# A fused mLSTM and feed-forward kernel on one core: the first steps' decay matrices by a triangular product and exp, three weight tensors signed by a Prelu slope, and a new order of the front

## The chip, the cores and the metric

The kernel runs on one core of a Trainium2 chip. Its engines are named as the profile names them: PE (TensorE, with PEld for its weight loads), DVE (VectorE), ACT (ScalarE), POOL (GpSimd) and SP (SyncE, which here only issues transfers). The metric is the device time of one run in microseconds, as the median of several runs. Beside it stands one profiled execution, from which every row comes.

## The reference

Two parts follow each other. The first is an mLSTM recurrence for 4 x 8 heads over 768 positions, with vectors of 40:

```python
m_new = np.maximum(f_gate[:, :, t] + m, i_gate[:, :, t])
f_stab = np.exp(f_gate[:, :, t] + m - m_new)
i_stab = np.exp(i_gate[:, :, t] - m_new)
C = f_stab * C + i_stab * outer(v, k);  n = f_stab * n + i_stab * k
y[:, :, t] = sigmoid(o_gate[:, :, t]) * (C @ q) / np.maximum(np.abs(n @ q), 1.0)
```

The second takes y as 3072 tokens of 320, and computes `softplus(x @ w_in) @ w_out` with 2048 hidden units. The two weight arrays arrive as 64-bit floats.

## The kernel before

The work is cut into 24 steps of 128 positions of one batch entry (8 heads each), and into 8 tiles of 3 steps. For each tile, `products` runs 16 blocks of 128 hidden units: eight matmuls of `wih`/`wil` with X into a bank `hp` (L1007), the softplus on ACT (L879 for tile 0, L883 after it), then the products with w_out into `po` (L978). There are three `hp` banks. X is the step's output, split into a high and a low part.

A step needs the decay from position s to position t, which is the product of f over the positions in between. `decay` (L449) gets it on DVE with one scan along t for four heads, from a row of f broadcast over the partitions and an identity that starts each row at 1. The scores are weighed with it (`weigh`, L584), `values` multiplies by the gated values (`vi`, L473, on POOL) into `yp` (L628), takes the reciprocal of the norm (`nq`), scales the output gate (`og`, L635, on POOL), writes `x` (L638, L639), and `split_x` transposes it (L733) and makes X high on ACT (L735) and X low on DVE (L737).

Weights are decoded from 64-bit words to single floats in `single`: ACT makes the magnitude (`mag`, L220), ACT or POOL takes the last three mantissa bits from the low word's top byte (`sg`, L225 or L228, by the parity of a number in `Q`), ACT writes the sign half (L230), and DVE joins the two (L233). Each w_in tensor is then split into a high part on ACT (L257, L261) and a low part on DVE (L265, L267). The first three tensors are decoded ahead of the products. Raw weights have three buffers.

What happens before the first product (the front) is `first_tile`: three steps whose pieces are emitted in the order of the numbers in the dictionary `F`. Every engine and the SP queue run their instructions in the order of emission. The pieces named below are `g0`, `g1` (the first gates: load, then the scan for m, the exps and the transpose of the input gate into `gT`), `lg0` to `lg2` (the gates of the later positions: load, scan, exp), `l0` to `l2` (q, k, v of a step), `f0` to `f2` and `sc0` to `sc2` (decay rows, scans), `s`, `m` (scores, weighing), `vi`, `v0a` to `v2c` (values), `x0a` to `x2c` (X), `wp` (one piece of the decoding of weights each), `wm` (seven warm-up matmuls), `o0s` and `o1s` (sigmoids of the output gates), `tsig` and `tab` (loads of ACT's function tables), `fz` (the decay rows of the first positions to DRAM, `gz_d`), and `zs` (zeros of state buffers, on POOL). In steps 0 and 1 the decay rows are broadcast by PE: one column of the identity, repeated, times `fg0`, per head (L437). Step 2 reads its rows back from `gz_d`.

After the first product, pieces are released by a count of matmuls n (a tile is 272 counts): steps 3 to 5 at `B3`, `B4`, `B5` with the offsets in `M`, later steps with those in `N` and `W`, and the decoding of the other weight tensors with `CI`, `CO`, `CS`, `K0`, `K1`.

Of the kernel before, what the change touches and what calls it, by code (L numbers as in the profile page):

```python
# [44 lines left out]
def mlstm_moe_kernel(  # L45
# [243 lines left out]
    W = dict(FB=-89, LOAD=-66, Y=-28, SCAN=10, VI=-5, VW=14, IQ=14, SP=23, SPD=12, CN=35, CD=36, CE=38, CF=68, YQ=52,  # L289
             YQD=4, EV=1, YD=66, YD1=-16, RD=96, RY=10, RZ=2, NM=132, FIN=137, XH=24, XL=4)  # L290
    M = dict(FB=-25, LOAD=-59, Y=13, SCAN=17, VI=-5, VW=17, IQ=37, SP=24, SPD=5, CN=35, CD=49, CE=54, CF=39, YQ=39,
             YQD=-22, EV=0, YD=41, YD1=-18, RD=85, RY=-6, RZ=0, NM=108, FIN=114, XH=8, XL=-4, CP=39)
    N = dict(FB=-26, LOAD=-59, Y=-6, SCAN=9, VI=-11, VW=11, IQ=23, SP=28, SPD=8, CN=30, CD=36, CE=38, CF=49, YQ=54,
             YQD=6, EV=1, YD=60, YD1=-4, RD=84, RY=-38, RZ=16, NM=125, FIN=150, XH=-9, XL=11)
    Q = dict(Gi0=-3, Go0=0, Gi1=0, Go1=1, Gi2=0, Go2=1, Gi3=0, Go3=17, Gi4=4, Go4=4, Gi5=-2, Go5=-1, Gi6=0, Go6=1,
             Gi7=0, Go7=1, B3=12, B4=71, B5=141, B6=232, B7=265, B8=372, B9=444, B10=525, S0=-377, S1=-292, S2=-199,
             GT=-393, GL=52, LB=217, LS=39, SPD=1, OF0=1, OF1=19, GR0=5, GR1=31, GR2=13, GR3=14, GR4=-3, GR5=27,
             LG=44, FS0=-23, FS1=-6, FSW=8, CI=-50, CO=-3, CS=34, K0=-8, K1=-17, CF=15, RC=-27, RS=95, B2=9, B11=617,
             GT2=92, GL2=106, FS2=0, GR6=-4)
    CI = dict(A=2, B=-14, C=6, D=24, E=19, F=32)  # L300
    CO = dict(A=18, B=-8, C=16, D=27, E=45)

    F = dict(wm=16, zs=212, g0=10, l0=19, w00=46, l1=51, g1=31, fz=63, o0=118, l2=116, lg0=7, f2=118, o1=122, o2=315,
             w10=210, w01=126, f0=163, s0=150, f1=146, s1=210, vi0=196, sc0=226, ld0=230, m00=254, m01=230, wp0=280,
             o0s=223, wp1=210, vi1=244, sc1=254, ld1=273, m10=285, m11=277, wp2=308, lg1=60, lg2=77, tsig=76,
             o1s=323, sc2=262, ld2=275, v0a=274, s2=317, v1a=312, v0b=358, tab=320, m20=330, v0c=404, m21=312,
             vi2=298, v2a=370, v1b=345, wp3=358, x0a=459, x0b=414, v1c=424, x1a=441, v2b=456, x0c=437, wp4=428,
             wp5=405, wp6=300, wp7=300, wp8=305, wp9=328, wp10=432, wp11=434, wp12=371, wp13=369, wp14=362, wp15=436,
             wp16=437, fetch2=348, fetch3=437, fetch=490, x1b=480, x1c=492, v2c=407, x2a=526, x2b=511, x2c=512,
             wr=512, sv0=526, sv1=536, sv2=660, tk6=153, tk5=155, tk4=160, tk3=165, tk2=162, tk1=174)  # L310
# [800 lines left out]
```

## Time and profile before

| what | us |
|---|---|
| median of 3 runs (471.85 to 472.82) | 471.95 |
| the profiled execution | 468.21 |
| its span, first to last instruction | 466.4 |
| PE busy in the span | 441.0 (95%) |
| DVE busy | 312.1 (67%) |
| ACT busy | 214.1 (46%) |
| POOL busy | 121.3 (26%) |

The busy times are means over the whole span. The front, which the change rewrites, is its first tenth, and there the shares are different. The profiled execution took 3.7 us less than the median of the other runs.

### The profile page before, as it was taken

What the parts mean: (1) busy time and instruction counts of PE and PEld (TensorE: products, weight loads), DVE (VectorE), ACT (ScalarE), POOL (GpSimd) and SP (SyncE); (2) the same over time, 40 slices, a digit from 0 to 9 for tenths busy, and PEclk for the clock granted to TensorE, in tenths of its full rate; (3) what the DMA queues carried; (4) which work ended last, traced back from release to release, by engine and by line L of the source; (5) the groups of instructions that cost most, each with busy time, mean ns of one, the idle gap of its engine ahead of it and who ended that gap; (6) DMA issues with size and microseconds to landing.
All of it is one profiled execution on the core that took longest, in us unless ns stands there. A gap on an engine that the chain in (4) does not pass through costs nothing.

```text
span 466.4 us, 10338 instructions
## 1 busy us (share of the span) xinstructions
PE 441.0 (95%) x4173; PEld 412.8 (89%) x4173; DVE 312.1 (67%) x585; ACT 214.1 (46%) x413; POOL 121.3 (26%) x137
## 2 busy tenths in 40 slices
PE   7487978998999999999999999999999999999997
PEld 6375866776999999999999999999999999999996
DVE  5855856989788877875776867756877687332121
ACT  5398557774343633354433633363334442433332
POOL 6415252546321332143031322212313111000000
PEclk9755998999999999999999999999999999999999
DMA  6948296977727643643562464354364220101001
GB/s 202 333 149 237 100 244 205 298 198 182 200 77 184 173 112 129 185 135 89 154 190 84 109 190 130 104 154 123 117 191 120 87 73 20 40 3 44 1 0 44
DMA packets 38399, 63.07 MB, mean 135 GB/s; under 512 B 5486, under 2 KB 20278, under 8 KB 38350
## 3 DMA queue, kind: packets, MB, share of 16 engines
q1 hardware_dynamic: 26218, 54.13, 39.8%
q10 hardware_dynamic: 12132, 8.26, 6.3%
q8 instruction: 33, 0.54, 0.5%
q14 instruction: 16, 0.13, 0.1%
HBM read 54.07 MB, written 8.31 MB: 134 GB/s over the span
## 4 chain that ended last, share of the span: by engine, by line
PE 72%; DMA 9%; DVE 8%; issue 4%; ACT 3%; SPq 1%; POOL 1%; ACTq 0%; DVEq 0%; POOLq 0%
PE hp L1007 33%; PE po L978 31%; PE yq L668 4%; DMA vt<-in_vko 2%; DMA yd<-y 2%; DMA gz_d<-fg 2%; PE sp L616 2%; PE sp L610 1%; DMA fc<-fc_d 1%; DMA yx<-yd 1%; DMA wi<-in_wts 1%; DVE pw L449 1%; DMA fb<-gz_d 1%; DVE nm L712 1%; ACT gh L883 1%
## 5 line engine op out<-in xcount | busy, mean ns | idle before, releaser
L1007 PE MATMUL hp<-X,wih 128*128 128x384 f32 x768 | 183.5, 346 | 3.2 <-ACT X L723 1.2
L1007 PEld LDWEIGHTS hp<-X,wih 128*128 128x128 f32 x768 | 135.5, 189 | 7.1 <-ACT X L723 1.6
L883 ACT ACTIVATE gh<-hp 128x384 fp32r<-128x384 f32 x112 | 55.1, 492 | 182.1 <-PE hp L1007 174.4
L887 DVE TENSOR_TENSOR gl<-hp,gh 128x384 fp32r<-128x384 f32 x112 | 61.7, 554 | 51.1 <-ACT hp L884 49.9
L978 PE MATMUL po<-woh,gl 128*128 128x320 f32 x336 | 72.2, 313 | 0.0
L978 PE MATMUL po<-wol,gh 128*128 128x320 f32 x336 | 71.2, 311 | 0.0
L978 PE MATMUL po<-woh,gh 128*128 128x320 f32 x336 | 70.2, 309 | 0.0
L1007 PE MATMUL hp<-X,wil 128*128 128x384 f32 x256 | 66.5, 341 | 0.0
L496 POOL TENSOR_TENSOR vw<-vt,gw 128x328 f32<-128x328 f32 x23 | 21.7, 944 | 144.5 <-DVE gw L487 137.8
L978 PEld LDWEIGHTS po<-woh,gh 128*128 128x128 f32 x336 | 57.3, 188 | 0.1
L978 PEld LDWEIGHTS po<-woh,gl 128*128 128x128 f32 x336 | 55.0, 189 | 0.6
L978 PEld LDWEIGHTS po<-wol,gh 128*128 128x128 f32 x336 | 54.5, 188 | 0.3
L884 ACT ACTIVATE hp<-hp 128x384 f32<-128x384 f32 x112 | 54.4, 486 | 0.0
L574 POOL TENSOR_TENSOR v<-v,flast 40x328 f32<-40x328 f32 x32 | 30.5, 953 | 63.7 <-DVE v L577 33.6
L1007 PEld LDWEIGHTS hp<-X,wil 128*128 128x128 f32 x256 | 46.8, 189 | 0.3
L621 DVE TENSOR_TENSOR mv<-sp,pw 64x256 f32<-64x256 f32 x72 | 27.2, 417 | 15.8 <-PE sp L616 15.5
L978 PE MATMUL po<-wof,gh 128*128 128x320 f32 x96 | 30.2, 459 | 4.4 <-DVE wof L233 4.4
L376 DVE TENSOR_TENSOR mv<-mv,fc 64x512 f32<-64x512 f32 (+1 forms) x36 | 31.0, 862 | 0.6
L478 POOL TENSOR_TENSOR v<-vt,gT 64x328 f32<-64x328 f32 x36 | 28.6, 794 | 9.0 <-DMA vt<-in_vko 6.5
L978 PEld LDWEIGHTS po<-wof,gh 128*128 128x128 f32 x96 | 18.5, 200 | 12.0 <-DVE wof L233 5.3
L725 DVE TENSOR_TENSOR X<-eg,X 128x384 fp32r<-128x384 f32 x21 | 12.2, 583 | 24.9 <-ACT X L723 24.8
L577 DVE TENSOR_TENSOR v<-v,sp 40x164 f32<-40x164 f32 x64 | 20.7, 323 | 2.4 <-POOL v L574 0.9
(133 smaller groups left out, 488.5 us busy)
## 6 DMA issues: line engine op xcount, KB each, us to landing
qk<-in_qk SPq DMA_DIRECT2D x21, 416.0 KB
vt<-in_vko SPq DMA_DIRECT2D x23, 324.0 KB
wi<-in_wts SPq DMA_DIRECT2D x8, 640.0 KB
wo<-in_wts SPq DMA_DIRECT2D x8, 640.0 KB
fb<-fz_d SPq DMA_DIRECT2D x36, 128.0 KB
eg<-in_oT SPq DMA_DIRECT2D x7, 576.0 KB
out<-ob SPq DMA_DIRECT2D x24, 160.0 KB
yd<-y ACTq DMA_DIRECT2D x36, 96.0 KB
```

Source lines behind the costliest of these rows:

```text
L376: nc.vector.tensor_tensor(z.mv[ch][r], z.mv[ch][r], z.fc[r], op=ALU.mult)
L478: nc.gpsimd.tensor_tensor(vi, v1[r], g[r], op=ALU.mult)
L496: nc.gpsimd.tensor_tensor(z.vw, v1, z.gw.broadcast_to([128, H, E]), op=ALU.mult)
L574: nc.gpsimd.tensor_tensor(heads(whole), old, f, op=ALU.mult)
L577: nc.vector.tensor_tensor(dst[i], dst[i], z.cps[ch][dims(i)], op=ALU.add)
L621: nc.vector.tensor_tensor(half(z.mv[ch][r], i), sps[i][r], half(z.pw[r], i), op=ALU.mult)
L668: nc.tensor.matmul(yq[i * PP : i * PP + m, p, rows(ch)], z.v[ch][k, h * E : h * E + m], z.mv[ch][k, h, :], start=True, stop=True,)
L883: nc.scalar.activation(gh, hp, AF.Softplus)
L884: nc.scalar.activation(hp, hp, AF.Softplus)
L887: nc.vector.tensor_tensor(gl, hp, gh, op=ALU.subtract)
L978: nc.tensor.matmul(po[j], a[:, j * 128 : (j + 1) * 128], w, start=first, stop=(last and left[j] == 0))
L1007: nc.tensor.matmul(hp, a, r, start=(i == 0), stop=(i == len(seq) - 1))
```

## The change

Decay matrices of steps 0, 1 and 2. The logarithm of f is transposed (`lT`). For each step and each half of the heads, POOL writes a tile that holds the logarithm of position s at all t not before s, and 0 elsewhere (`affine_select`, pieces `r`). PE multiplies it by a strictly triangular matrix `later`, which sums the logarithms, ACT takes the exp, and POOL sets the other half to 0 (pieces `e`). The scans, the broadcasts by PE, and step 2's trip through `gz_d` are gone. The steps take their next pieces from one generator, so the four of a step run in the order of their numbers, whatever their names.

Weights. For the three tensors decoded ahead, `mag` is a Prelu whose slope puts the sign into the exponent's top bit; the third ACT instruction goes. For the others, the low parts of w_in can go to POOL by the parity of `H` and `J` in `Q`; three pairs (`Ji0`, `Ji2`, `Ji4`) do.

Order. The new numbers put the load of the first gates first in the SP queue, `lg0`, all of the steps' loads, the output gates and two weight tensors behind it, the selects and exps of all three steps ahead of all scores, `tsig` behind the last exp, and `o1s` ahead of `tab`. So the tables are loaded once each. `zs` goes behind the third X. The numbers of the later steps change a little, and with `EV=-1` the copy of `y` in steps 3 to 5 goes from DVE to ACT.

```diff
+    later = p1.tile([128, 4, 128], F32, tag="fc", name="later")[:, 0]
+    nc.gpsimd.memset(later, 1.0)
+    nc.gpsimd.affine_select(
+        later, later, pattern=[[-1, 128]], compare_op=ALU.is_gt, fill=0.0, base=0, channel_multiplier=1
+    )
...
+        nc.vector.memset(fg[:, 0:1], 0.0)
         nc.scalar.activation(ig, ig, AF.Exp)
+        pg = ps_a.tile([128, 2, NCHAIN], F32, tag="pa", name="pg0")
+        nc.tensor.transpose(pg[:, 1], fg, ident[:NCHAIN, :NCHAIN])
+        nc.tensor.transpose(pg[:, 0], ig, ident[:NCHAIN, :NCHAIN])
+        nc.scalar.copy(lT, pg[:, 1])
+        nc.scalar.copy(gT[:, 0, :], pg[:, 0])
+        done.add(("gT", 0))
+        yield
         nc.scalar.activation(fg, fg, AF.Exp)
         nc.vector.memset(fg[:, 0:1], 0.0)
         done.add("fg0")
-        pg = ps_a.tile([128, NCHAIN], F32, tag="pa", name="pg0")
-        nc.tensor.transpose(pg, ig, ident[:NCHAIN, :NCHAIN])
-        nc.scalar.copy(gT[:, 0, :], pg)
-        done.add(("gT", 0))
         yield
...
-        nc.scalar.activation(mag, hi_w.bitcast(F32), AF.Copy, scale=2.0**-112)
+        if slope:
+            nc.scalar.activation(mag, hi_w.bitcast(F32), AF.Prelu, scale=2.0**-112, alpha=-(2.0**32))
+        else:
+            nc.scalar.activation(mag, hi_w.bitcast(F32), AF.Copy, scale=2.0**-112)
...
+        if slope:
+            nc.scalar.activation(sg, top, AF.Copy, scale=1.0 / 32, bias=-31.0 / 64)
+        elif Q["G" + n] % 2:
...
-        nc.scalar.activation(half[:, :, 1], hi_w.bitcast(F32), AF.Copy, scale=2.0**-112)
-        yield
+        if not slope:
+            nc.scalar.activation(half[:, :, 1], hi_w.bitcast(F32), AF.Copy, scale=2.0**-112)
+            yield
...
-        nc.vector.tensor_tensor(wil[:, :, cs], w2, wih[:, 0:2, cs], op=ALU.subtract)
+        e0, e1 = (nc.gpsimd if Q[k + f"i{u}"] % 2 else nc.vector for k in "HJ")
+        e0.tensor_tensor(wil[:, :, cs], w2, wih[:, 0:2, cs], op=ALU.subtract)
         for d, x, y in los:
-            nc.vector.tensor_tensor(d, x, y, op=ALU.subtract)
+            e1.tensor_tensor(d, x, y, op=ALU.subtract)
...
+    M = dict(FB=-25, LOAD=-47, Y=3, SCAN=14, VI=-15, VW=17, IQ=31, SP=24, SPD=21, CN=35, CD=51, CE=67, CF=45, YQ=39,
+             YQD=-50, EV=-1, YD=45, YD1=-15, RD=85, RY=-27, RZ=0, NM=113, FIN=114, XH=8, XL=-4, CP=39)
...
+    F = dict(wm=140, zs=820, g0=-20, l0=12, w00=118, l1=88, g1=145, fz=297, o0=109, l2=85, lg0=82, f2=226, o1=308,
+             o2=684, w10=181, w01=298, f0=192, s0=304, f1=224, s1=308, vi0=364, ld0=328, m00=352, m01=361, wp0=444,
+             o0s=437, wp1=492, vi1=368, ld1=365, m10=368, m11=369, wp2=499, lg1=244, lg2=280, tsig=423, o1s=726,
+             ld2=396, v0a=448, s2=399, v1a=468, v0b=473, tab=750, m20=398, v0c=492, m21=408, vi2=418, v2a=548,
+             v1b=492, wp3=503, x0a=515, x0b=560, v1c=524, x1a=594, v2b=586, x0c=603, wp4=552, wp5=577, wp6=588,
+             wp7=576, wp8=664, wp9=665, wp10=712, wp11=699, wp12=746, wp13=765, wp14=851, wp15=862, wp16=877,
+             fetch2=685, fetch3=764, fetch=572, x1b=589, x1c=623, v2c=591, x2a=700, x2b=685, x2c=706, wr=850,
+             sv0=774, sv1=782, sv2=780, tk6=720, tk5=760, tk4=728, tk3=784, tk2=812, tk1=810, r0=178, r1=180, r2=183,
+             e00=196, e01=188, e10=227, e11=236, e20=246, e21=246, g2=278)
...
-            need("fg0" if z.s < 2 else ("gz", z.c))
+            need(("gz", z.c))
             z.fbs = []
             for i in range(2):
-                if z.s >= 2:
-                    fb = p2.tile([128, HG, L], F32, tag="fb", name=f"fb{z.n}_{i}")
-                    nc.sync.dma_start(fb, gz_d[z.c, z.hs].rearrange("(i p) t -> i p t", i=2)[i].partition_broadcast(128))
-                    z.fbs.append(fb)
-                    continue
-                fb = ps_h.tile([128, HG, L], F32, tag="hp", name=f"fb{z.n}_{i}")
-                for j in range(HG):
-                    h = z.b * H + i * HG + j
-                    nc.tensor.matmul(
-                        fb[:, j, :], ident[:, h : h + 1].broadcast_to([128, 128]), fg0, start=True, stop=True
-                    )
+                fb = p2.tile([128, HG, L], F32, tag="fb", name=f"fb{z.n}_{i}")
+                nc.sync.dma_start(fb, gz_d[z.c, z.hs].rearrange("(i p) t -> i p t", i=2)[i].partition_broadcast(128))
                 z.fbs.append(fb)
...
+    def first_decays(z):
+
+        need(("gT", 0))
+        z.pws = []
+        keep = dict(compare_op=ALU.is_ge, fill=0.0, base=0, channel_multiplier=-1, pattern=[[0, HG], [1, L]])
+        for i in range(2):
+            pw = p2.tile([128, HG, L], F32, tag="pw" if z.s < 2 else "fb", name=f"pw{z.n}_{i}", **({"bufs": 4} if z.s < 2 else {}))
+            g = half(lT[:, z.hs], i).unsqueeze(2).broadcast_to([128, HG, L])
+            nc.gpsimd.affine_select(pw, g, **keep)
+            z.pws.append(pw)
+        yield
+        fbs = []
+        for i in range(2):
+            fb = ps_h.tile([128, HG, L], F32, tag="hp", name=f"fb{z.n}_{i}")
+            nc.tensor.matmul(fb, later, z.pws[i], start=True, stop=True)
+            fbs.append(fb)
+        yield
+        for i in range(2):
+            nc.scalar.activation(z.pws[i], fbs[i], AF.Exp)
+            nc.gpsimd.affine_select(z.pws[i], z.pws[i], **keep)
+            yield
...
+            done.add("softplus")
...
+            yield from (weights_out if i else weights)(u, words and "softplus" not in done)
```

## Rows read from the trace of the kernel before

**Rows 1.** Page, 40 slices of the span: busy tenths of PE, TensorE clock granted.
```profile
PE   7487978998999999999999999999999999999997
...
PEclk9755998999999999999999999999999999999999
```

**Rows 2.** Windows: us; busy time of PE, PEld, DVE, ACT, POOL; clock, DMA share, GB/s.
```profile
80.00:100.00 20.00, 18.19 (x126) 14.28 (x127) 18.25 (x32) 16.31 (x29) 10.15 (x8) 1.00 0.81 253
```

**Rows 3.** Waits of PE, 39 to 140 us: us in total, times, longest.
```profile
PE po L978 <- DVE wof L233: 4.4, 3, 2.5
```

**Rows 4.** Timeline, 0 to 25 us: start us, us, engine, line, op, idle before.
```profile
1.19 0.41 SPq L158 DMA_DIRECT2D ig<-in_gates  x1
...
2.10 0.42 SPq L133 DMA_DIRECT2D ig<-in_gates  x1
...
2.49 3.35 PE L750 MATMUL wm<-ident 128*128 128x128 f32 x14 [2.49 <-POOL ident L78]
...
3.95 0.47 DVE L136 TENSOR_TENSOR_SCAN m<-fg,m,ig 32x128 f32<-32x128 f32 x1 [2.95 <-DMA ig<-in_gates]
...
6.12 0.19 ACT L147 COPY gT<-pg 128x32 f32<-128x32 f32 x1 [0.33 <-PE pg L146]
...
6.33 1.28 ACT L790 ACT_TABLE_LOAD   x1
...
7.61 1.28 ACT L167 ACT_TABLE_LOAD   x1
...
9.76 1.16 PE L437 MATMUL fb<-fg,ident 128*128 128x128 f32 x8
...
15.67 1.95 PE L628 MATMUL yp<-vi,pw 128*128 128x41 f32 x16 [1.11 <-DVE pw L584]
```

**Rows 5.** Groups by shape, 0 to 46 us, POOL: busy us, mean ns, idle before.
```profile
L85 POOL TENSOR_SCALAR_AFFINE_SELECT near<-near 128x512 f32<-128x512 f32 x2 | 1.3, 660 | 0.1
...
L165 POOL TENSOR_TENSOR ig<-ig,m 32x640 f32<-32x640 f32 x1 | 1.9, 1941 | 3.9 <-DVE m L162 3.9
...
L473 POOL TENSOR_TENSOR vi<-vt,gT 128x328 f32<-128x328 f32 x2 | 1.5, 737 | 1.0 <-DMA vt<-in_vko 0.9
...
L473 POOL TENSOR_TENSOR vi<-v,gT 128x328 f32<-128x328 f32 x1 | 1.3, 1306 | 0.0
```

**Rows 6.** Groups by shape, 0 to 46 us, DVE.
```profile
L449 DVE TENSOR_TENSOR_SCAN pw<-fb,ident 128x512 f32<-128x512 f32 x6 | 7.2, 1218 | 2.3 <-PE fb L437 2.0 <-DMA fb<-gz_d 0.2
...
L233 DVE SCALAR_TENSOR_TENSOR sgi<-magi,sgi 128x640 uint32<-128x640 uint32 x3 | 2.5, 817 | 1.7 <-ACT sgi L230 1.7
...
L638 DVE TENSOR_TENSOR x<-yp,og 128x320 f32<-128x320 f32 x3 | 2.2, 717 | 0.6 <-POOL og L635 0.6
...
L265 DVE TENSOR_TENSOR wil<-sgi,wih 128x512 fp32r<-128x512 f32 x2 | 1.4, 688 | 0.7 <-ACT wih L257 0.7
...
L639 DVE COPY x<-x 128x64 f32<-128x64 f32 x3 | 1.1, 353 | 0.1
...
L634 DVE RECIPROCAL nq<-nq 128x8 f32<-128x8 f32 x3 | 0.6, 203 | 0.1
```

**Rows 7.** Groups by shape, 0 to 46 us, ACT.
```profile
L230 ACT ACTIVATE sgi<-wi 128x640 f16<-128x640 f32 x3 | 2.7, 904 | 0.0
...
L765 ACT ACTIVATE eg<-eg 128x1152 f32<-128x1152 f32 x2 | 2.2, 1154 | 0.0
...
L735 ACT CAST X<-xp 128x384 fp32r<-128x384 f32 x3 | 1.4, 468 | 0.8 <-PE xp L733 0.8
```

**Rows 8.** Timeline, 25 to 50 us: first products, first softplus.
```profile
29.14 3.61 PE L628 MATMUL yp<-vi,pw 128*128 128x41 f32 x16 [0.87 <-DVE pw L584]
...
39.68 0.69 PE L1007 MATMUL hp<-X,wih 128*128 128x384 f32 x1 [0.57 <-DMA wi<-in_wts]
...
45.30 0.49 ACT L879 ACTIVATE gh<-hp 128x384 f32<-128x384 f32 x1
...
47.94 1.20 PE L1007 MATMUL hp<-X,wih 128*128 128x384 f32 x6
```

More of the change, by code (lines that the diff above doesn't have):

```diff
@@ L98, in mlstm_moe_kernel @@
     m_end = cpool.tile([NCHAIN, 1], F32, name="m_end")
-    fg0 = cpool.tile([128, L], F32, name="fg0")
+    fg0 = cpool.tile([NCHAIN, L], F32, name="fg0")
+    lT = cpool.tile([128, NCHAIN], F32, name="lT")
     done = set()
@@ L126, in first_gates @@
     def first_gates():
-        nc.vector.memset(fg0, 0.0)
-        fg = fg0[:NCHAIN]
+        fg = fg0
         ig = p1.tile([NCHAIN, L], F32, tag="sig", name="ig0")
@@ L211, in mlstm_moe_kernel, with single @@
     wof, wol = [None] * (NF // 2), [None] * (NF // 2)
-    def single(raw, n, dst=None):
+    def single(raw, n, dst=None, slope=False):
         if not words:
@@ L248, in load_weights, with weights @@
         raw[u, i] = r
-    def weights(u):
+    def weights(u, slope=False):
         cs = slice(u * 256, (u + 1) * 256)
-        w = yield from single(raw[u, 0], f"i{u}")
+        w = yield from single(raw[u, 0], f"i{u}", None, slope)
         w = w.rearrange("p (c f) -> p c f", f=128)
@@ L264, in weights, with weights_out @@
         yield
-        nc.vector.tensor_tensor(wil[:, :, cs], w2, wih[:, 0:2, cs], op=ALU.subtract)
+        e0, e1 = (nc.gpsimd if Q[k + f"i{u}"] % 2 else nc.vector for k in "HJ")
+        e0.tensor_tensor(wil[:, :, cs], w2, wih[:, 0:2, cs], op=ALU.subtract)
         for d, x, y in los:
-            nc.vector.tensor_tensor(d, x, y, op=ALU.subtract)
+            e1.tensor_tensor(d, x, y, op=ALU.subtract)
         done.add(("wi", u))
         yield
-    def weights_out(u):
+    def weights_out(u, slope=False):
         wof[u] = wl.tile([128, 2, DM], F32, tag="wo", name=f"wof{u}")
-        w = yield from single(raw[u, 1], f"o{u}", wof[u].rearrange("p j e -> p (j e)") if words else None)
+        w = yield from single(raw[u, 1], f"o{u}", wof[u].rearrange("p j e -> p (j e)") if words else None, slope)
         done.add(f"o{u}")
@@ L287, in lows @@
             yield -1000 - Q["LS"]
[L289 to L293, printed above, removed]
-             YQD=6, EV=1, YD=60, YD1=-4, RD=84, RY=-38, RZ=16, NM=125, FIN=150, XH=-9, XL=11)
@@ L295, in mlstm_moe_kernel @@
[L295 to L310, printed above, removed]
+    W = dict(FB=-89, LOAD=-66, Y=-28, SCAN=4, VI=-5, VW=14, IQ=15, SP=25, SPD=12, CN=35, CD=36, CE=38, CF=68, YQ=52,
+             YQD=-12, EV=1, YD=66, YD1=-16, RD=96, RY=10, RZ=2, NM=132, FIN=137, XH=24, XL=4)
@@ new lines, in mlstm_moe_kernel @@
+    CI = dict(A=-3, B=3, C=-36, D=24, E=8, F=32)
+    CO = dict(A=6, B=-27, C=15, D=26, E=4)
+    F = dict(wm=140, zs=820, g0=-20, l0=12, w00=118, l1=88, g1=145, fz=297, o0=109, l2=85, lg0=82, f2=226, o1=308,
[7 more added lines that the diff above has]
+             e00=196, e01=188, e10=227, e11=236, e20=246, e21=246, g2=278)
@@ L774, in keep_decays @@
             need("fg0")
-            nc.sync.dma_start(gz_d[0], fg0[:NCHAIN])
+            nc.sync.dma_start(gz_d[0], fg0)
             done.add(("gz", 0))
@@ L786, in first_tile @@
         ev = dict(
-            wm=warm, zs=zeros, g0=lambda: next(p0), g1=lambda: run(p0), fz=keep_decays,
+            wm=warm, zs=zeros, g0=lambda: next(p0), g1=lambda: next(p0), g2=lambda: run(p0), fz=keep_decays,
             o0=lambda: next(o0), o0s=lambda: next(o0), o1=lambda: next(o1), o2=lambda: next(o1), lg0=lambda: next(lg), lg1=lambda: next(lg),
@@ L799, in first_tile @@
             ev[f"l{i}"] = lambda z=z: load(z)
-            ev[f"f{i}"] = lambda z=z: decays(z)
+            d = first_decays(z)
+            ev[f"r{i}"] = lambda g=d: next(g)
+            ev[f"f{i}"] = lambda g=d: next(g)
+            ev[f"e{i}0"] = lambda g=d: next(g)
+            ev[f"e{i}1"] = lambda g=d: next(g)
             ev[f"vi{i}"] = lambda z=z: gate_values(z)
-            ev[f"sc{i}"] = lambda z=z: decay(z)
             ev[f"ld{i}"] = lambda z=z: last_decays(z)
@@ L946, in ahead @@
         for u, i in tensors[:AHEAD]:
-            yield from (weights_out if i else weights)(u)
+            yield from (weights_out if i else weights)(u, words and "softplus" not in done)
     wparts = ahead()
```

8 lines of the change are left out of this document (7 added, 1 removed).

## The prediction

> **What bounds the kernel now.** I read the page's 40 slices first. PE is full from about the eleventh slice to the end, at full clock [rows 1]. So nothing that the change does to the later tiles can show, unless it makes a wait there; a gain or a loss must come out of the first 120 us, and it lasts if PE reaches the full stretch that much earlier or later. I then read the timeline from 0 to 50 us. The first matmul of the products starts at 39.68, and the fourth block's matmuls (the first that need a bank `hp` back from ACT) begin in the row at 47.94, about 48.1 [rows 8]. Ahead of that PE is partly idle and mostly at half its clock (slices 3 and 4 of rows 1). Last I read what is tight behind the start: from 80 to 100 us DVE is busy 18.25 of 20 us, ACT 16.31, and the DMA engines 0.81 of the time [rows 2]; PE's largest wait up to 140 us is 4.4 us for decoded w_out [rows 3]. The front sets the start, then, and what runs beside tile 0 has little room.
>
> **The change: what it removes.** Six scans of 1.22 us on DVE, 7.3 us [rows 6]; three sign halves on ACT, 3 x 0.90 = 2.7 us [rows 7]; step 2's trip through DRAM. Of the table loads two stand back to back at 6.33 and 7.61 [rows 4], as does another pair later; in the new order exp, sigmoid and softplus are loaded once each, so four of seven loads of 1.28 us go, 5.1 us of ACT. None of these is the sum by itself, since DVE and ACT also wait in the front. So I follow the new chain.
>
> **The chain, first leg: to the selects.** The second load of the first gates is issued at 2.10 and the scan starts 1.85 us later, at 3.95. Issued second instead of fourth (1.19), it lets the scan start at 3.04. That gives nothing yet: the transposes stand behind the warm-up on PE, which ends at 2.49 + 3.35 = 5.84, and the copy to `gT` came at 6.12 to 6.31 before [rows 4]. `lT` is copied in its place; POOL can begin at about 6.4. The set-up of `later` on POOL (a memset and a select a quarter as wide as the rows of 0.66) falls into the time before that.
>
> **Second leg: POOL.** Twelve selects of 128x512, at the row's 0.66, are 7.9 us. Between the first ten and the last two stands the subtraction of `lg1` (1.94), and behind them `vi` of step 0, 0.74 [rows 5]. 6.4 + 7.9 + 1.94 + 0.74 = 17.0. One `vi` took 1.31 beside DVE's work on the later gates, 0.57 more than the others [rows 5], and the first selects now run beside that same work. Bounds: nothing, and all six first selects slowed in that proportion, 6 x 0.66 x 0.77 = 3.1 us. I take 1.0, as that work on DVE is only a few instructions: 18.0. That a select with a broadcast input costs what one in place does is not in any row; it is the slower rival below.
>
> The Trainium skill (GPSIMD Engine Reference, section 3, performance versus the Vector engine) gives 769 ns as measured for a tight loop over 512 elements on this engine, above the row's 660. By it the twelve selects would take 1.3 us longer, and the time below would be 465.0.
>
> What this leg hides: the sums on PE (the same columns as the broadcasts that they replace, 1.16 us for a half [rows 4]) and exps on ACT, 0.58 each between the casts of 384 and the sigmoids of 1152 columns [rows 7]. Step 0's first exp is done near 6.4 + 0.66 + 1.16 + 0.58 = 8.8, and POOL comes to it at 6.4 + 6 x 0.66 = 10.4. If the cover is gone, a late exp costs up to 0.58. Scores and weighing of all steps fall between 12 and 18; so do exps for the later gates, the table load and the sigmoid of `og`, on ACT. The loads of all three steps are in the SP queue ahead of every wait; `fz`, which waits for the last gate exp, holds only a third weight tensor and the next gates, needed much later.
>
> **Third leg: values.** `yp` of step 0 took 1.95 at full clock [rows 4] and a like one 3.61 at half [rows 8]. PE was at full clock before when it had worked as it now will until then; I take 1.95, with 1.7 more as the other end: 20.0.
>
> **Fourth leg: DVE's list up to the third x.** `nq` is three instructions of up to 0.20, 0.6; `x` is 0.72 + 0.35; a join is 0.82; `wil` 0.69 [rows 6]; `og` on POOL is as wide as `vi`, 0.74. In the order of the new numbers: nq 0.6, og 0.74, x 1.07, nq 0.6, join 0.82, x 1.07, wil 0.69, nq 0.6, join 0.82, x 1.07: 8.1, so 28.1. Three transposes at half clock (0.9, an estimate from the 1.16 for eight at full clock [rows 4]) and the cast of X high, 0.47 [rows 7]: 29.4. For some ten hand-overs between engines at about 0.1 I add 1.0: the first product at 30.4, 9.3 earlier than 39.68.
>
> **Fifth leg: what is late next.** Before its first softplus ACT has the third tensor's `sg`, both sigmoids of 1.15, a table load, and five decoding instructions at up to 0.90 [rows 4, 7]: 0.9 + 2.3 + 1.3 + 4.5 = 9.0, so 39.4, with the softplus itself of 0.49 [rows 8] 39.9. PE alone, at the pace of before (48.1 - 39.7 = 8.4), would want the bank at 38.8. So the fourth block starts at 39.9, and 48.1 - 39.9 = 8.2 us of the gain are left.
>
> The table loads that stand back to back take 1.28 each with nothing between them [rows 4]. The Trainium skill (ScalarE: Activation LUTs, What ACT_TABLE_LOAD costs) adds a drain of 1.38 us to every switch, 2.66 in all; by it the first softplus would come 1.4 us later and the time would be 465.1. The row shows no such gap.
>
> **Work moved behind the start.** The zeros on POOL are needed only by the first states' copies. Three pairs of low parts go from DVE to POOL, and three copies of `y` from DVE to ACT, in the stretch where DVE is the fullest. The shifted offsets of later steps act on a PE that is full. I cost all this at nothing: 4.4 us [rows 3] is the most that it can give back, and the rival of the head start is what it costs if the cover fails.
>
> Sum: 8.2 us off. The profiled execution would go from 468.2 to 460.0; the runs' median, 3.7 above it, from 471.95 to 463.7.
>
> **The rivals.**
> *The head start is lost* (0.17). The products begin 8.2 us earlier, but raw weights, decay rows and values for steps 3 to 5 still have to be brought and decoded beside tile 0. For it speaks the DMA share of 0.81 with DVE at 0.91 and ACT at 0.82 [rows 2]. If transfers can catch up only in their idle share of that stretch, 0.19 x 20 = 3.8 us, the gain is 3.8: 468.1. Against it: before, too, all of it was released by the count n, and DMA had slack at other times.
> *Tile 0's own waits go too* (0.13). The new parities take the waits for w_out of rows 3 away: 463.7 - 4.4 = 459.3, and less where the clock also rises sooner.
> *The selects are slow: slower than before* (0.09). A select from a broadcast column, or in place beside DVE, may cost more than 0.66. Twelve stand on the path, so it decides from 0.66 + 8.2/12 = 1.34 us each, which is what `vi` took when slowed, on fewer columns. At 1.31 x 512/328 = 2.04 the chain grows by 16.6 us: 472 + 8.4 = 480. Against it: both in-place selects of that size took 0.66.
> *No change* (0.03). The decays come sooner, but the first product waits for something else that has not moved, such as the decoding of the first tensor. Then 472. Against it: its raw words have landed before the chain asks for them, and its instructions are in the list above.
>
> **How the numbers follow.** The forecast has 0.58, with a range of its own from 460.5 (no contention, hand-overs at half, the clock up sooner) to 467.5 (all of the contention and `yp` at half clock). About 0.2%, 0.9 us, is what a measurement of this kernel can tell from no change. Faster is 0.58 + 0.17 + 0.13 = 0.88, the same 0.03, slower 0.09. The range from 457.5 to 469.5 takes in the two neighbours for the larger part, and leaves out the two cases at the other side.
>
> **What would show it.** In the changed kernel: twelve selects near 0.66; `yp` of step 0 near 18; no scan ahead of step 3; three table loads before the first softplus; the first product near 30 and the fourth block near 40; tile 0 as long as before. The prediction is wrong if selects come at 1.3 or more, if ACT holds the softplus past 45, or if PE's waits between 40 and 120 grow by more than 4 us.

## The result, and the profile after

| kernel | median of the runs, us | lowest to highest | runs |
|---|---|---|---|
| before | 471.49 | 467.68 to 473.64 | 20 |
| after | 470.0 | 461.82 to 473.13 | 20 |

The ratio is 0.9885, with an interval from 0.9851 to 0.9918: faster by 1.1%, where 1.7% had been forecast (463.7 from 471.95). It is made from the runs within 1.5% of each kernel's fastest, which are all of before's and eight of after's, so it flatters the kernel with the wider spread: on before's median it stands for 466.1 us, inside the range from 457.5 to 469.5, while the plain median of all twenty lies 0.5 us above that range and only 0.3% under before's. Medians stand beside ratios below. The profiled run of after took 471.93 (span 470.2), one of the longer ones; before's took 468.21, one of its shortest, so the two traces are compared stretch by stretch and not by their ends. The spread of after is itself a result: the six runs with a mean granted clock of 0.970 or more took 461.8 to 468.8 us, the fourteen at 0.967 or less 467.2 to 473.1.

The page of after, 40 slices of 11.8 us: busy tenths of PE and the granted clock.

```profile
PE   6788889986999999999999999999999999999997
...
PEclk9857798999999999999999999999999999999999
```

Before, the clock was low in the third and fourth slices and up from the fifth [rows 1]. In after it is low from the third to the fifth. By narrower windows these are, up to 60 us, two dips: from about 21 to 41 us, shorter than before's (about 18 to 45), and a second one behind 51 us, at which before was at full clock.

The timeline of after, 0 to 9 us (start, duration, engine, line, instruction, idle before):

```profile
3.17 0.59 DVE L141 TENSOR_TENSOR_SCAN m<-fg,m,ig 32x128 f32<-32x128 f32 x1 [2.25 <-DMA ig<-in_gates]
...
6.43 0.18 ACT L151 COPY lT<-pg 128x32 f32<-128x32 f32 x1 [1.22 <-PE pg L150]
...
6.68 2.40 POOL L468 TENSOR_SCALAR_AFFINE_SELECT pw<-lT 128x512 f32<-128x512 f32 x4 [2.46 <-ACT lT L151]
```

The scan starts at 3.17 (forecast 3.04) and the selects at 6.68 (6.4), after the copy of `lT`. The groups of POOL by shape from 0 to 46 us (busy us, mean ns):

```profile
L468 POOL TENSOR_SCALAR_AFFINE_SELECT pw<-lT 128x512 f32<-128x512 f32 x6 | 5.3, 928 | 2.5 <-ACT lT L151 2.5
L479 POOL TENSOR_SCALAR_AFFINE_SELECT pw<-pw 128x512 f32<-128x512 f32 x6 | 4.2, 725 | 0.0
...
L174 POOL TENSOR_TENSOR ig<-ig,m 32x640 f32<-32x640 f32 x1 | 1.3, 1307 | 0.0
...
L504 POOL TENSOR_TENSOR vi<-v,gT 128x328 f32<-128x328 f32 x1 | 0.7, 725 | 0.0
```

The twelve selects took 5.3 + 4.2 = 9.5 us, not 7.9; the subtraction of `lg1` took 1.31, not 1.94 [rows 5]. So `vi` of step 0 ended at 18.10, against 18.0 forecast. What did not follow is `yp`. The same timeline, 14 to 24 us:

```profile
14.92 1.31 POOL L174 TENSOR_TENSOR ig<-ig,m 32x640 f32<-32x640 f32 x1
...
15.20 1.05 DVE L521 TENSOR_TENSOR gw<-gT,pw 128x4 f32<-128x4 f32 x1 [2.52 <-POOL pw L479]
...
16.18 2.65 DVE L521 TENSOR_TENSOR gw<-gT,pw 128x4 f32<-128x4 f32 x1
16.19 1.21 POOL L479 TENSOR_SCALAR_AFFINE_SELECT pw<-pw 128x512 f32<-128x512 f32 x2
...
17.38 0.72 POOL L504 TENSOR_TENSOR vi<-v,gT 128x328 f32<-128x328 f32 x1
18.07 1.42 POOL L504 TENSOR_TENSOR vi<-vt,gT 128x328 f32<-128x328 f32 x2
...
18.75 1.27 DVE L615 TENSOR_TENSOR pw<-sp,pw 128x512 f32<-128x512 f32 x2
...
19.48 2.06 PE L626 MATMUL sp<-qk 40*128 40x128 f32 x16 [3.15 <-DVE pw L615]
19.95 0.23 DVE L521 TENSOR_TENSOR gw<-gT,pw 128x4 f32<-128x4 f32 x2
...
21.47 2.78 PE L659 MATMUL yp<-vi,pw 128*128 128x41 f32 x12
```

The reader is to compare two forms of one instruction. The product `gw` (128x4, piece `ld0`) takes 1.05 and 2.65 us while POOL works without a gap, and 0.23 for two at 19.95, when POOL has stopped. Behind it on DVE stands the weighing, which starts at 18.75; behind the weighing, on PE, the scores of step 2, which wait 3.15 us for a bank; behind those `yp`, at 21.47 instead of 18.17 or so. Further on, 24 to 48 us:

```profile
28.99 3.48 PE L659 MATMUL yp<-vi,pw 128*128 128x41 f32 x16
...
37.00 0.69 PE L1042 MATMUL hp<-X,wih 128*128 128x384 f32 x1 [0.57 <-ACT X L766]
...
37.55 2.21 ACT L796 ACTIVATE eg<-eg 128x1152 f32<-128x1152 f32 x2
...
39.77 1.28 ACT L810 ACT_TABLE_LOAD   x1
...
45.73 0.49 ACT L914 ACTIVATE gh<-hp 128x384 f32<-128x384 f32 x1
...
46.27 1.14 PE L1042 MATMUL hp<-X,wih 128*128 128x384 f32 x5 [1.12 <-ACT gh L914]
```

The values run at half the clock. The first product comes at 37.00 (39.68 before, [rows 8]), the fourth block at 46.27 (48.1), so the profiled run is 1.8 us ahead there. It loses that in tile 0: tile 1's first product is at 113.63, against 109.92 before, so the stretch between took 67.4 us instead of 61.8. PE's waits from 25 to 140 us in after, the longer ones, show only a part of that:

```profile
PE po L1013 <- DVE wof L248: 3.1, 2, 1.7
...
PE hp L1042 <- ACT X L754: 2.2, 1, 2.2
PE po L1013 <- ACT chain L568: 1.8, 1, 1.8
...
PE hp L1042 <- ACT gh L914: 1.1, 1, 1.1
```

The waits for w_out are 3.1 us, where they were 4.4 [rows 3]; the wait of 1.8 for ACT's copies of the state is new, and the one for X just before tile 1 is 2.2 instead of 1.2. (The wait of 1.1 for `gh` is the one that ends at the fourth block.) In all, PE is idle for 8.0 of the 67.4 us and was for 6.1 of the 61.8: 1.9 of the 5.6 us. In the other 3.7 PE is busy for longer, 59.4 us instead of 55.7, with the same products. The windows of the same run show why (us; busy time of PE, PEld, DVE, ACT, POOL; clock, DMA share, GB/s):

```profile
30.00:40.00 10.00, 7.20 (x40) 5.81 (x40) 7.62 (x16) 8.84 (x16) 8.55 (x14) 0.50 0.34 97
40.00:50.00 10.00, 7.90 (x75) 6.36 (x74) 4.06 (x5) 8.38 (x16) 6.52 (x6) 0.94 0.99 322
50.00:60.00 10.00, 9.14 (x52) 6.20 (x53) 6.00 (x13) 3.26 (x9) 4.04 (x5) 0.66 0.16 42
45.00:110.00 65.00, 58.06 (x369) 44.76 (x369) 46.99 (x74) 43.35 (x82) 32.24 (x31) 0.92 0.72 210
```

Half clock (1.2 GHz, 0.50 in the rows) holds from about 21 to 41 us, and returns for most of 51 to 59 us, where PE is busy. From 45 to 110 us, nearly all of tile 0, the mean is 0.92; before it was 0.97.

### The profile page after: what moved, and what is told of

The parts are those of the page before. It is cut to its first block, busy times and chain, and to the rows that moved or that the text cites. A ratio compares the mean times of both kernels' runs of the same rounds, so it can differ in the third digit from the quotient of the medians.

```text
span 470.2 us, 10336 instructions
## 1 busy us (share of the span) xinstructions
PE 446.5 (95%) x4154; PEld 413.1 (88%) x4154; DVE 308.3 (66%) x570; ACT 211.6 (45%) x415; POOL 136.6 (29%) x158
## 4 chain that ended last, share of the span: by engine, by line
PE 84%; POOL 4%; ACT 3%; DVE 3%; DMA 3%; issue 2%; SPq 1%; POOLq 0%; ACTq 0%; DVEq 0%
PE hp L1042 36%; PE po L1013 35%; PE yq L699 4%; PE yp L659 2%; DMA qk<-in_qk 2%; PE sp L647 2%; PE sp L641 2%; POOL pw L468 1%; PE sp L626 1%; PE yq L684 1%; DMA mv<-in_q 1%; PE wm L781 1%; DVE pw L458 1%; POOL sgi L239 1%; POOL pw L479 1%
## 5 line engine op out<-in xcount | busy, mean ns | idle before, releaser
L1042 PE MATMUL hp<-X,wih 128*128 128x384 f32 x768 | 181.0, 344 | 6.5 <-ACT X L754 2.2
L1013 PE MATMUL po<-wol,gh 128*128 128x320 f32 x336 | 69.8, 309 | 0.0
L1042 PE MATMUL hp<-X,wil 128*128 128x384 f32 x256 | 68.9, 346 | 0.0
L1013 PE MATMUL po<-wof,gh 128*128 128x320 f32 x96 | 32.1, 483 | 4.9 <-DVE wof L248 3.1
L394 DVE TENSOR_TENSOR mv<-mv,fc 64x512 f32<-64x512 f32 (+1 forms) x36 | 32.0, 889 | 0.6
L509 POOL TENSOR_TENSOR v<-vt,gT 64x328 f32<-64x328 f32 x36 | 27.2, 756 | 11.2 <-DMA vt<-in_vko 8.6
L717 ACT COPY y<-yq 112x512 f32<-112x512 f32 x21 | 12.3, 588 | 27.9 <-PE yq L699 22.0
```

The source lines that it names most:

```text
L394: nc.vector.tensor_tensor(z.mv[ch][r], z.mv[ch][r], z.fc[r], op=ALU.mult)
L509: nc.gpsimd.tensor_tensor(vi, v1[r], g[r], op=ALU.mult)
L717: (nc.scalar.copy if z.at["EV"] % 2 else nc.vector.tensor_copy)(z.y, yq)
L1013: nc.tensor.matmul(po[j], a[:, j * 128 : (j + 1) * 128], w, start=first, stop=(last and left[j] == 0))
L1042: nc.tensor.matmul(hp, a, r, start=(i == 0), stop=(i == len(seq) - 1))
```

## The experiments

Theory A: the small products on DVE, held while POOL works, delay the weighing, and with it all that follows. Theory B: the clock alone does it, since PE is idle between 16 and 19 us, and the delay of the weighing would cost little if the clock stayed up. Theory C: the offsets and parities of the later steps lose in tile 0 what the front gains. All times are medians of all runs; the ratio is to before on the same chip. The chips differ: there, before has medians of 470.4 (e0, e1, e3, e4), 471.15 (e5 to e8) and 471.12 us (e2, e9 to e11), so across chips the ratios are the ones to compare. "Fourth" is the start of the fourth block, "tile 0" the time from there to tile 1's first product, "clock" the mean granted from 45 to 110 us, these and the first product from one profiled run.

| run | median | lowest to highest, runs | ratio and interval | first product | fourth | tile 0 | clock |
|---|---|---|---|---|---|---|---|
| before | 471.49 | 467.68 to 473.64, 20 | | 39.68 | 48.1 | 61.8 | 0.97 |
| after | 470.0 | 461.82 to 473.13, 20 | 0.9885 [0.9851, 0.9918] | 37.00 | 46.27 | 67.4 | 0.92 |
| e0_again | 470.67 | 463.58 to 473.19, 12 | 0.9932 [0.9892, 0.9972] | 38.29 | 47.58 | 66.5 | 0.92 |
| e1_gw_late | 462.98 | 462.69 to 467.36, 6 | 0.9874 [0.9832, 0.9916] | 31.57 | 40.84 | 63.2 | 0.97 |
| e9_two_operands | 468.81 | 465.65 to 470.65, 12 | 0.9965 [0.9934, 0.9996] | 38.30 | 47.56 | 66.7 | 0.92 |
| e10_one_operand | 468.82 | 465.09 to 471.08, 12 | 0.9959 [0.9934, 0.9985] | 37.57 | 46.85 | 62.8 | 1.00 |
| e2_fill | 467.02 | 465.77 to 467.89, 8 | 0.9939 [0.991, 0.9968] | 35.27 | 44.54 | 63.1 | 1.00 |
| e3_both | 465.61 | 463.95 to 467.5, 6 | 0.9903 [0.9869, 0.9937] | 31.95 | 41.24 | 65.1 | 0.95 |
| e11_decode_later | 469.35 | 467.54 to 491.36, 12 | 0.9969 [0.9939, 0.9999] | 34.26 | 42.97 | 70.0 | 0.92 |
| e4_old_numbers | 468.08 | 462.76 to 470.97, 12 | 0.9927 [0.9892, 0.9962] | 37.61 | 47.31 | 63.0 | 0.97 |
| e5_gw_old_numbers | 463.07 | 460.75 to 467.38, 6 | 0.9835 [0.9788, 0.9882] | 31.24 | 40.91 | 62.4 | 1.00 |
| e6_tables_alone | 472.31 | 468.17 to 473.63, 12 | 1.0006 [0.9978, 1.0033] | 39.33 | 47.25 | 63.3 | 0.95 |
| e7_gw_no_slope | 465.04 | 463.06 to 467.11, 6 | 0.9869 [0.9834, 0.9904] | 31.42 | 41.21 | 62.8 | 0.97 |
| e8_scans | 471.51 | 469.25 to 474.65, 12 | 1.0015 [0.9982, 1.0047] | 39.63 | 48.93 | 63.6 | 1.00 |

**e0_again.** The changed kernel, unedited.

> The changed kernel once more, for a second trace of it and for its time beside the kernel before on one chip. In its first trace the first product came at 37.0 us, where 30.4 was forecast, and tile 1 began at 113.6, 3.7 later than in the kernel before. Theory A: the front is late because the first weighing waits for a small product on DVE that POOL holds up, and because the values' matmuls then run at half clock; both are there in every run, so the first product comes near 37 again, and the end is a matter of the stretches at half clock in tile 0, which change from run to run (450 to 462 for the last product). Theory B: tile 0 hands back whatever the front gains, because its decoding cannot be earlier: tile 1 begins near 113 again, whatever the clock. Ratio to the kernel before: 0.985 to 0.997 by A, 0.997 to 1.003 by B.

470.67 for 470.4 of before on this chip, with the same spread, and a ratio of 0.9932 where after had 0.9885: by its median the change alone is worth little here. Tile 0 is long again, 66.5 us.

**e1_gw_late.** ACT copies the last columns of the decay matrices, which frees the products from the place ahead of the weighing; they follow it.

```diff
+    def keep_last(z):
+        z.gl = p2.tile([128, H, 1], F32, tag="gl8", bufs=3, name=f"gl{z.n}")
+        for i in range(2):
+            nc.scalar.copy(half(z.gl, i), z.pws[i][:, :, L - 1 : L])
...
-    ld0=328, ld1=365, ld2=396
+    lc0=247, lc1=248, lc2=397, ld0=410, ld1=411, ld2=412
```

> As the changed kernel, but the last columns of the first three steps' decay matrices are copied by ACT, and the product with the input gate follows the weighing on DVE, so that no product of two SBUF operands stands ahead of the weighing. Theory A: the first weighing starts near 15.4 instead of 18.75, the values of step 0 near 18.2 instead of 21.5 and the first product at 33.5 to 35; with PE at full clock when the values begin, up to 31. The time falls by 2 to 4 us against the changed kernel. Theory B: the first product comes as much earlier, but tile 1 begins within 1 us of the changed kernel's, and the time stays.

Its timeline, 15 to 43 us:

```profile
15.55 3.69 DVE L624 TENSOR_TENSOR pw<-sp,pw 128x512 f32<-128x512 f32 x6
...
18.17 4.93 PE L668 MATMUL yp<-vi,pw 128*128 128x41 f32 x32
...
19.16 0.53 DVE L521 TENSOR_TENSOR gw<-gT,gl 128x8 f32<-128x8 f32 x3
...
31.57 0.69 PE L1052 MATMUL hp<-X,wih 128*128 128x384 f32 x1 [0.57 <-ACT X L775]
...
40.30 0.49 ACT L924 ACTIVATE gh<-hp 128x384 f32<-128x384 f32 x1
...
40.84 1.15 PE L1052 MATMUL hp<-X,wih 128*128 128x384 f32 x5 [0.36 <-ACT gh L924]
```

All six weighings are done at 19.24, beside the same selects on POOL; `yp` starts at 18.17, 0.06 after `vi` of step 0. The first product comes 5.4 us earlier than in after, and the median is 7.0 us under after and 7.7 under e0_again on the same chip. A is as good as confirmed, but the edit also changes the order on ACT. So the hold was put back by itself.

**e9_two_operands** and **e10_one_operand.** Both are e1 with two instructions of 128x4 on DVE ahead of the weighing, whose results nobody reads: products of two operands in SBUF, or a scale and add of one operand.

```diff
+            for i in range(2):
+                nc.vector.tensor_tensor(d, gT[:, 0, 0:HG], gT[:, 0, HG : 2 * HG], op=ALU.mult)   # e9
+                nc.vector.tensor_scalar(d, gT[:, 0, 0:HG], 0.5, 1.0, op0=ALU.mult, op1=ALU.add)  # e10
```

> The kernel with the product with the input gate behind the weighing (first product 31.6, median 463.0), with two small products of two SBUF operands (128x4 each, their result is read by nobody) on DVE ahead of the first weighing, while POOL runs its selects and the gated values. If it is POOL's hold on products of two SBUF operands that made the changed kernel late, these two take 2 to 4 us together instead of 0.3, the values of step 0 begin at 20 to 22, and the time goes back up by 3 to 7 us, to 466 to 470. If the late start came from somewhere else, such as the wait for the selects, the time stays at 463 within 1.

> The same with two small instructions of one SBUF operand (128x4 each) at the same place. If only products of two SBUF operands are held, these take 0.15 us or less each, the values of step 0 begin at 18.2 to 18.6, and the time stays at 463 within 1. If any DVE instruction on SBUF is held, they take as long as the two products and the time goes up alike.

DVE in e9, then in e10, from 15 to 20 us:

```profile
16.29 2.53 DVE L795 TENSOR_TENSOR gd<-gT 128x4 f32<-128x4 f32 x1 [3.60 <-issue]
...
19.44 2.47 DVE L624 TENSOR_TENSOR pw<-sp,pw 128x512 f32<-128x512 f32 x4
```

```profile
15.41 0.83 DVE L795 TENSOR_SCALAR gd<-gT 128x4 f32<-128x4 f32 x1 [2.74 <-issue]
15.42 0.06 DVE L156 MEMSET fg<- 32x1 f32 x1
...
16.27 2.54 DVE L795 TENSOR_SCALAR gd<-gT 128x4 f32<-128x4 f32 x1
...
18.72 2.47 DVE L624 TENSOR_TENSOR pw<-sp,pw 128x512 f32<-128x512 f32 x4
```

Either pair brings the wait back, the first product to 38.30 and 37.57, and the median to 468.8; the ratios, 0.9965 and 0.9959, lie clear of e1's 0.9874. That shows A. The first of e10's two cases, that only two operands are held, falls: one operand in SBUF waits as long. The memset (0.06 at 15.42) and the weighing, which reads one operand from PSUM, are not held. The Trainium skill (GPSIMD Engine Reference, Specifications) says that the two engines share SBUF interfaces, and that DVE instructions with two SBUF inputs, or in a mode that uses both ports, contend with this engine. The held forms fit it, if the one-operand form runs in such a mode, which no run here shows; the size of the wait, 2.5 us for four columns, is in the rows alone.

**e2_fill.** After, the hold kept, with five wide matmuls of the identity, whose results nobody reads, on PE ahead of step 2's scores.

```diff
+                nc.tensor.matmul(wm, ident, ident4, start=True, stop=True)   # five times, F: fa=309
```

> The changed kernel with the small products where they were, and five wide matmuls of the identity (nobody reads them) on PE between the scores of steps 1 and 2, where PE was idle from 16.3 to 19.5. If the clock were the cause of the late first product, keeping PE busy there keeps it at full for the values (2 us each instead of 3.6) and brings the first product from 37 or 38 to 33 to 34, and the time to 464 to 467. If the cause is the hold on DVE and the list of DVE behind the values, the values still begin at 21 to 22.5 and the first product comes at 35 to 37.5, with the time within 2 us of the changed kernel's 470.

A window of e2, and its timeline at 16 us:

```profile
20.00:25.00 5.00, 5.00 (x44) 4.12 (x42) 3.44 (x12) 0.68 (x2) 0.30 (x1) 0.94 0.79 260
```

```profile
16.18 2.65 DVE L521 TENSOR_TENSOR gw<-gT,pw 128x4 f32<-128x4 f32 x1
...
16.36 4.56 PE L786 MATMUL fill<-ident 128*128 128x512 f32 x10
```

The hold stays at 2.65, the clock is at 0.94 from 20 to 25 us (half from 21 us in after), and the first product comes at 35.27: 1.7 us of what after lost at that point, out of 5.4. The median is 3.0 under after's, between the two cases of the expectation. So B has a part, but a smaller one.

**e3_both.** e1 with the same filler in three places between the values.

> As the one with the product behind the weighing, and five extra wide matmuls of the identity (nobody reads them) between and behind the values' matmuls of steps 0, 1 and 2, so that PE is not idle there. Theory A: the clock stays at full from 15 to the first product, the values' matmuls take 2 us each instead of 3.6, the first product comes at 29 to 32, and the time falls by 4 to 8 us against the changed kernel. If the clock falls all the same, the extra matmuls cost up to 1.7 us each and the first product comes at 36 to 40. Theory B: the time stays within 2 us of the changed kernel's, wherever the first product is.

A window of e3, and its fourth block:

```profile
20.00:30.00 10.00, 9.03 (x53) 6.35 (x52) 6.15 (x17) 5.27 (x10) 5.21 (x6) 1.00 0.54 176
```

```profile
41.24 1.14 PE L1060 MATMUL hp<-X,wih 128*128 128x384 f32 x5 [1.56 <-ACT gh L932]
```

With the clock at 1.00 through all values the first product is at 31.95, no earlier than e1's 31.57. The filler has a price of its own (`nq` of step 1 starts at 24.02, in e1 at 23.14), so e3 does not show what the full clock alone would give. e1's rows give an idea of it: DVE waits 0.50, 0.49 and 0.47 us there for the three steps' values, so a faster PE had little more than 1.5 us to give ahead of the first product (an estimate). At the fourth block it only waits: 1.56 us for `gh`, behind ACT's list.

**e11_decode_later.** e1 with two of the decoding pieces that ACT does before its first softplus released later.

```diff
-    K0=-30, K1=-16
+    K0=12, K1=16
```

> The kernel with the product with the input gate behind the weighing, with the decoding of the fourth and fifth weight tensors released 12 and 16 counts after the first product instead of at once. ACT then has one decoding instruction ahead of its first softplus instead of four. If ACT's queue is what holds the fourth block, as the fifth leg says, the first softplus comes at 37 to 38 instead of 40.4, the fourth block at 38.5 to 39.5 instead of 40.8, and tile 1 up to 2 us earlier: 461 to 463. If the decoding itself is what tile 0 waits for, the waits for decoded weights grow by as much and the time stays or rises, 463 to 466.

```profile
PE po L1023 <- ACT chain L577: 5.4, 1, 5.4
```

```profile
47.80 0.92 ACT L245 ACTIVATE sgi<-wi 128x640 f16<-128x640 f32 x1 [6.84 <-POOL sgi L239]
```

PE's waits, and this row of ACT, show what happened. There is no wait for `gh` at the fourth block, and from the first product to the first softplus it is 6.2 us (34.26 to 40.47) instead of 8.7, so ACT's list had held it, as the fifth leg says. But the pieces that were put off now stand ahead of ACT's copies of the state: ACT waits 6.84 us for POOL's part of the decoding (which stands behind a `vi` that waited 7.9 us for its load), PE 5.4 us for the copies, and tile 0 takes 70.0 us. In this run the clock was at 0.50 from 17 us on already (first product 34.26), so the loss is not all the edit's.

**e4_old_numbers** and **e5_gw_old_numbers.** After, and e1, with the offsets and parities (`W`, `M`, `N`, `Q`, `CI`, `CO`) of before, and all low parts on DVE.

> The changed kernel's front with all numbers of the later steps and of the decoding as in the kernel before (engine choices too: copies of y in steps 3 to 5 on DVE, low parts of w_in all on DVE). The front must be as in the changed kernel, first product near 37. Theory A: what tile 0 loses comes from idle time and half clock there, and the old numbers lose it in the same way or a little differently: time within 3 us of the changed kernel's. Rival C: the new numbers themselves cost it (tile 0 took 76.6 us instead of 70.2): with the old ones tile 1 begins near 107 and the time falls by 4 to 6 us.

> The changed kernel with the product with the input gate behind the weighing (the edit that took the first product to 31.6 and the median to 463.0) and with the old numbers for all later steps and the decoding (the edit that took the changed kernel from 470.7 to 468.1). If both losses are separate, tile 0 takes 63 from its fourth block to tile 1 as with the old numbers alone, tile 1 begins near 102 and the time is 459.5 to 462. If the new numbers fit the earlier start (tile 0 took as long with them once the start was early), the time stays at 462 to 465.

With the hold, the old numbers have the lower median by 2.6 us (468.08 and 470.67 on one chip), but the ratios' intervals cover each other. Without the hold, e5 (463.07) and e1 (462.98), on two chips, can't be told apart, by their ratios either. So C is not shown: if the new numbers cost anything, it is where the front is late.

**e6_tables_alone.** Before, with the two table loads moved so that four loads go (`tsig=78`, `tab=324`).

> The kernel before with nothing but the order of its table loads changed: the sigmoid table behind the exps of the later gates, the softplus table behind the sigmoids of the output gates, so that four of seven loads go, 5.1 us of ACT. If the loads were on the chain to the first product, it comes 2 to 3 us earlier than 39.7 and the time falls by 2 to 3 us. If, as in the forecast, they are not, since DVE and PE wait for other things, the first product stays within 1 us of 39.7 and the time within 1 us; the first softplus may come up to 2.6 us earlier.

Ratio 1.0006 with an interval of 0.3% either way. Three loads of 1.28 us are left of seven, and the first softplus came 1.7 us sooner (43.64 against 45.30, [rows 8]), but the first product hardly moved (39.33 against 39.68) and the time did not follow.

**e7_gw_no_slope.** e1, with the sign half as a third instruction for the three tensors again.

```diff
-            nc.scalar.activation(mag, hi_w.bitcast(F32), AF.Prelu, scale=2.0**-112, alpha=-(2.0**32))
+            nc.scalar.activation(mag, hi_w.bitcast(F32), AF.Copy, scale=2.0**-112)
...
+            nc.scalar.activation(half[:, :, 1], hi_w.bitcast(F32), AF.Copy, scale=2.0**-112)
```

> The changed kernel with the product with the input gate behind the weighing, and the three tensors decoded ahead without the slope: the third instruction on ACT is back, in one piece with the second, so that the order is the same. 3 x 0.9 us more on ACT. ACT is idle for 3 us before the first join, but the second tensor's join and the third tensor's decoding stand close to the chain: first product at 31.6 to 33, first softplus 1 to 2.7 later than with the slope, time 0 to 2 us above 463.0. If the slope had no part in it, 463.0 within 0.5.

First product 31.42 against 31.57, fourth block 41.21 against 40.84, ratios 0.9869 and 0.9874 (medians 465.04 and 462.98, on two chips): the slope has no part that can be measured with six runs of each.

**e8_scans.** After's order, with the decays by the broadcasts on PE and six scans on DVE, as before.

> The changed kernel with its decay matrices made as before: broadcasts by PE and six scans on DVE (all three steps from PE), at the places of the selects and exps in the new order. No selects on POOL, so the small products are not held up, but DVE has 7.3 us of scans and 5 us for the later gates ahead of the weighing: weighing of step 0 at 19 to 20.5, values of step 0 at 21 to 22, first product at 36 to 37.5, time as the changed kernel's, 468 to 472. If the triangular product is what moved the first product, it comes at 39 or later here and the time is 1 to 3 us longer; if the product costs more than it gives (POOL's hold on DVE), the first product comes at 33 to 35 and the time falls to 464 to 467.

```profile
15.14 3.21 DVE L169 TENSOR_TENSOR fg<-fg,m 32x640 f32<-32x640 f32 x1
18.28 2.32 DVE L454 TENSOR_TENSOR_SCAN pw<-fb,ident 128x512 f32<-128x512 f32 x2
...
24.10 2.14 PE L652 MATMUL yp<-vi,pw 128*128 128x41 f32 x9
```

Ratio 1.0015: the new order without the triangular product gains nothing. Here DVE's last two scans come behind a subtraction of 32x640 that takes 3.21 us beside POOL's products for the values (0.81 for the like one just before it, at 14.29; 1.14 for L173 in after), and the values start at 24.10. So in this order, which was made for it, the gain needs the triangular product. As POOL's hold costs this run some 2.4 us too, what the scans would do in an order of their own is not shown.

## Why the prediction was right in direction and off in size

*First and second leg: right in sum, in part by luck.* 3.17 and 6.68 for 3.04 and 6.4, and `vi` of step 0 done at 18.10 for 18.0. Two terms were off and cancelled: the selects took 9.5 us for 7.9 + 1.0, the subtraction 1.31 for 1.94. Of the first six selects, four took 0.60 each (2.40 us for four), and the two beside DVE's work on the later gates 5.3 - 2.4 = 2.9 us together; the first select in place was slowed as well, to 1.2. The mean over twelve, 0.79, is far from the 1.34 that the rival of slow selects needed.

*The failed step.* "Scores and weighing of all steps fall between 12 and 18" was given as cover for the second leg. The weighing began at 18.75 and ended at 22.95. The prediction charged contention between DVE and POOL to POOL alone, 1.0 us, and had no entry for the small products on DVE, 152 ns each before. Ahead of the weighing they cost 3.2 us (18.75 against 15.55 in e1). No rival named it: it is a wait that the change itself makes, by filling POOL without a gap. The old trace had a sign that POOL holds DVE too. Of two like subtractions on DVE the second, beside POOL's product on 32x640 (7.63 to 9.57), took 1 us more:

```profile
7.58 0.81 DVE L163 TENSOR_TENSOR fg<-fg,m 32x640 f32<-32x640 f32 x1
...
8.43 1.82 DVE L164 TENSOR_TENSOR fg<-fg,m 32x640 f32<-32x640 f32 x1
```

*Third leg: right without the hold, wrong with it.* `yp` of step 0 was to run from 18.0 to 20.0. In e1 it starts at 18.17, and `nq` follows its end at 20.18. In after it starts at 21.47, behind the fall of the clock, and ends at 25.15: 3.3 us late by the hold, 1.7 by the clock. That second price was in the prediction as the other end of its term, the first was not. The idle time of PE from 16 to 19 us is not all of the fall's cause: in e1, where PE is busy for 5.7 of the 6 us up to 20, the clock falls at about the same time, 20.5, but `yp` of step 0 is through by then.

*Fourth leg: undersized by about 1 us.* From the end of `yp` to the first product the forecast had 30.4 - 20.0 = 10.4 us; e1 has 31.57 - 20.18 = 11.4, e3 at full clock, with its filler, the same, after 37.00 - 25.15 = 11.9. In e1, too, the two engines slow each other behind the weighing:

```profile
27.82 1.21 POOL L675 TENSOR_TENSOR og<-og,nq 128x320 f32<-128x320 f32 x1 [0.89 <-POOL wih L283]
...
29.06 0.74 DVE L678 TENSOR_TENSOR x<-yp,og 128x320 f32<-128x320 f32 x1 [0.61 <-POOL og L675]
```

`og` of steps 1 and 2 takes 1.19 and 1.21 us beside a join on DVE (0.72 alone, in step 0), and DVE then waits 0.61 us for it, twice: 1.2 us, where the forecast had `og` hidden behind the join.

*Fifth leg: right.* From the first product to the first softplus 9.0 us were forecast, 8.73 measured in after as in e1. The fourth block at 39.9 is at 40.84 in e1: without the hold, 7.3 of the 8.2 us that were forecast there are gained, with it 1.8. e1's median, 462.98, comes close to the forecast's 463.7, but its profiled run is only 5.2 us under before's (463.01 and 468.21): 2.1 of the 7.3 us are lost again, in tile 0 and behind it. So the chain to the fourth block holds without the hold; that the median meets the forecast as well is partly luck.

*Work moved behind the start: little with an early front, 5.6 us in after.* Tile 0 was costed as long as before. e1 and e5 need 63.2 and 62.4 us for it (61.8 before), after 67.4. Most of the extra goes with the clock: the four runs with 0.92 from 45 to 110 us (after, e0_again, e9, e11) need 66.5 to 70.0, all those at 0.95 or more 61.8 to 65.1. PE is busy for 59.3 to 59.5 us of tile 0 in these four, for 55.2 to 56.0 in before, e1, e5 and e10. Why the clock falls again near 51 us in some of the runs stays open: in after PE had just waited 1.8 us for ACT's state copies, but e1 waits 1.9 at the same place in its products without a fall, and e10, as late at its start as after and with the same wait, doesn't show one (62.8). Both traces of the changed kernel have this second dip; that it makes the spread between its runs is likely by their mean clocks, but not shown. The rival of the lost head start gave 468.1 and comes close to the median, by another mechanism: up to 140 us none of PE's listed waits is for a transfer.

*The range.* Of the signs that the prediction named, the selects (0.79 each, well short of 1.3) and the three table loads came; `yp` near 18, the first product near 30, the fourth block near 40 and a tile 0 as long as before did not, and the first softplus at 45.73 is past its mark of 45, because the first product was late and not by ACT's list. That the ratio lies in the range all the same is luck more than mechanism: neither trace of the changed kernel takes the forecast's path.

*Tables and slope: right that none is the sum by itself.* Neither has a part that could be measured (e6, e7).

The better version is e1, or e5: 463 us, 1.3 to 1.7% under before by their ratios, and under the change by their medians.

## What to carry to other kernels

When work is moved to POOL, list what DVE does beside it, the shortest instructions first: a product of four columns, 0.15 us in the old trace, took 2.65 us at the head of a queue on which weighing, scores and values depended. Move such an instruction behind the work that is waited for. A delay in the front can be paid twice, as itself and by moving matmuls into a stretch at half clock (3.3 and 1.7 us for `yp` here). Filling PE's gap put that stretch off in e2, but it is worth only what the next list (here DVE's, then ACT's) does not take.
